# A delta-rule recurrence and a gated MLP on one core: own places for the first gates, and three dense products per batch inside the recurrence where there were five

## The chip, the cores and the metric

The kernel runs on one core of one Trainium2 chip. The metric is the device time of one execution in microseconds (us); it is 695.72 us, the median of three runs of the kernel before. Every duration below comes from a profiled execution of the same kernel.

## The reference

Two stages follow each other. The first is a recurrence over 768 time steps for 4 batches of 8 heads, with a 40x40 state per head:

```python
for t in range(S):
    y[:, :, t] = np.einsum('bhd,bhde->bhe', rt, state)
    Sa = np.einsum('bhde,bhe->bhd', state, at)
    state_decay = state * wt[:, :, None, :] - np.einsum('bhd,bhe->bhde', Sa, bt)
    state = state_decay + np.einsum('bhd,bhe->bhde', vt, kt)
```

Its output, with the heads side by side, is x of shape (4, 768, 320). The second stage is a gated MLP on x: h = gelu(x @ w_in) with 1024 columns, split into u and v of 512; v is normalized over its columns, multiplied with a 768x768 matrix over time (v_s = w_sg v_n + b_sg), and the result is x + (u * v_s) @ w_out.

## The kernel before

**The recurrence in chunks.** Time is cut into 12 chunks of 64 steps. Inside a chunk the steps are solved as a 64x64 triangular system per head. Each chunk has two halves f (two batches each), and each half has two kinds of work.

The *gate* of a half (gate_1 to gate_n, lines 313 to 372) doesn't depend on the state. DVE scans the decays (two scans into `ex`), multiplies them into `at`, and forms `kb` in two parts (a reciprocal, a scan and a product each). PE then multiplies `kb` with `at` into `ab` (gate_s) and transposes `kb` into `kt` (gate_t); ACT copies the negated blocks of `ab` into `nts` (gate_n) and `kt` into `kbt` (gate_k), and DVE masks `ab` back into `at` (gate_a). The inputs of a gate, `main`, have two buffers; gate_3's end releases the load for the gate after next.

The *inverse* of the triangular blocks is made for a whole group of chunks: DVE transposes `nts` into `n` in 32x32 blocks (inv_in), POOL does 58 small multiplications and additions into `tg` and `x`, one column after the other (inv_sub), DVE does the last two columns (inv_end) and transposes `x` into `x1z` (inv_turn). The groups are chunk 0, chunk 1, and then pairs (2, 3), (4, 5) up to (10, 11). `n` has one buffer, so the next group's transposition follows the last group's end.

The *chain* of a chunk (inv_back, inv_g, inv_x, chain1 to chain5) needs that inverse and the state of the chunk before. It runs over PE, ACT and DVE in turn (`xt`, `ru`, `us`, `vu`, `ut`, `pq`, `pqs`, `sp`, `sc`, `yp`, `yt`), and stores the chunk of x to DRAM (`xd`).

**The order is written out by hand.** Every piece of this work has a position, a number. YC gives the position of a chunk's chain, YG the origin of its gates, GATE the offsets of a gate's eleven pieces, YI and INV (INV1 for single chunks) those of a group's inverse. `at_` collects the pieces, in_order sorts them and holds a piece back while the PSUM bank that it would take is in use; each engine then issues its instructions in that order, and the DMA queue SP likewise. A position is thus no time: it says only what stands ahead of what.

**The dense products.** A v-product takes 128 rows of x and the v-half of w_in. Both operands are split into two fp32r parts (`xh`, `xl`; `wvh`, `wvl`), and eight matmuls of 512 columns add up in one bank. Before the change five of the six v-products of each batch are laid into the recurrence: as soon as two chunks of x are done, fill_x loads them (`xf`), fill_split (ACT) and fill_low (POOL) split them (`xfh`, `xfl`), fill_v multiplies (PE, bank `hf`), and fill_out copies the raw product (ACT, `hv`) and stores it to DRAM (`hd`). fill_low also stores the split x to DRAM (`xhd`, `xld`). LASTF is their number, FILL their offsets in a chunk. The v-weights are loaded and split ahead of them, in six pieces at the positions DEC (wstep, line 1050): a load, an activation on ACT, four integer operations on DVE, a copy on ACT, and three subtractions, on DVE for one piece and on POOL for the next.

**The dense half.** Behind the recurrence run issues the rest: u-products (`hu`), the remaining v-products (`hv`), products over time (`sg`) and output products (`op`), by the list FIRSTS for batch 0 and SEQ for each batch. For a v-product that is done already it loads the raw product and does only the gelu and the normalization. GELU, normalization and gates are on ACT, DVE and POOL (`p`, `v`, `bs`, `vh`, `vl`, `g`, `gy`, `gx`), and follow a product by one or two products (later, tick). At a batch's beginning split_x makes the split x of the next batch: for its first 640 columns it loads `xhd` and `xld`, for the last 128 it splits on ACT and DVE. PF are the positions at which batch 0's five products get their gelu while the recurrence still runs.

Of the kernel before, what the change touches and what calls it, by code (L numbers as in the profile page):

```python
# [34 lines left out]
HI_MIN = float(np.uint32(896 << 20).view(np.float32))  # L35
HI_MAX = float(np.uint32(1151 << 20).view(np.float32))
WARM = 14
WARMS = ((-4.831, 8), (-4.331, 8))
BLANKS = -21.0
ZEROS = -36.0  # L40
LOADS = -24.0
PER = 25.5
LATE = 2.5
STORE = 1.5
GATE = ((-101.908, -100.107, -99.028, -96.184, -97.801, -95.604, -92.188, -90.251, -93.577, -91.478, -91.823),
    (-93.163, -92.271, -89.673, -85.987, -88.462, -85.151, -80.147, -78.616, -83.325, -79.712, -81.287))
CHAIN = ((0.0, 1.942, 2.468, 5.095, 5.152, 6.489, 14.151, 16.047, 17.757, 7.942, 9.521, 12.185, 14.84, 17.073,
    19.654), (11.001, 12.574, 2.94, 4.267, 13.405, 14.279, 15.32, 18.186, 26.426, 16.496, 19.044, 24.204, 26.192,
    29.01, 31.005))
YC = (0, 27.5, 81.0, 106.5, 132.0, 157.5, 183.0, 208.5, 234.0, 259.5, 285.0, 310.5)  # L50
YG = (35.908, 55.908, 81.0, 106.5, 132.0, 157.5, 183.0, 208.5, 234.0, 259.5, 285.0, 310.5)
YI = (-3.831, 23.669, 81.0, 132.0, 183.0, 234.0, 285.0)
GATEE = {(0, 0): "VG", (0, 1): "GG"}
GROUPS = ((0,), (1,), (2, 3), (4, 5), (6, 7), (8, 9), (10, 11))
LAST = 2
NBANK = 6
INV = (-61.011, -53.011, -50.811, 0.759, -6.51, -5.143)
INV1 = (-44.0, -29.3, -27.1, 0.429, -2.0, -1.3)
BACK = (-3.831, -0.954, -1.454, -2.595, -0.449, 1.071, 3.249)
END_GT = 232.184  # L60
END_IW = 279.907
END_RING = 292.105
END_IV = 314.249
CG = 0.7978845608028654
G1 = 0.044715
PIN = 232.194
DSTEP = ((-8.5, -1.0, 0.0, 0.7, 1.4, 2.4), (-8.5, -1.0, 0.0, 0.7, 1.4, 2.4))
DSTEPF = (-2.5, -0.5, 0.0, 0.7, 1.4, 2.4)
DEC = (5.0, 15.0, 25.0, 35.0, 45.0, 55.0, 241.194, 247.194, 253.194, 259.194, 265.194, 271.194)
GE = "VV"  # L70
FILL = ((-9.701, 2.299, 2.749, 5.899, 8.777), (3.497, 15.497, 15.947, 19.922, 22.61))
FILLG = True
LASTF = 5
PX = 314.449
PXS = 314.459
PV = 292.205
PS = 338.954
PL = 331.954
PF = (303.0, 308.0, 313.0, 318.0, 323.0)
PH = 9  # L80
FILLERS = ("v0", "v1", "v2", "v3", "v4")
FIRSTS = ("u1", "u0", "u2", "u3", "v5", "u4", "u5", "u6", "u7")
SEQ = ("s1", "s2", "s0", "s3", "s4", "v0", "s5", "v1", "o0", "o1", "o2", "s6", "s7", "v2", "u0", "v3", "u1", "v4",
    "v5", "o3", "o5", "o4", "u2", "u3", "u4", "u5", "u7", "u6")
XS = 0
REST = 8
HL = 2
SGS = (5, 3, 5, 6, 7, 8, 8, 11, 10, 11, 12, 11)
PO = 232.204
DECO = (277.194, 283.194, 289.194, 295.194, 301.194, 307.194, 313.194, 319.194)  # L90
# [102 lines left out]
def attention(tc, a, xd, flag, keep, ps, mlp=None):  # L193
# [4 lines left out]
    with ExitStack() as ctx:  # L198
# [419 lines left out]
            at_(LOADS, load_rv, 0, f)  # L618
        for c in range(NCH):
            for f in range(2):  # L620
                y, n = YG[c], GATE[f]
                at_(y + n[0], gate_1, c, f, 0)
                at_(y + n[1], gate_1, c, f, 1)
                at_(y + n[2], gate_2, c, f, E={"V": V, "G": G}[GATEE.get((c, f), GE)[0]])
                at_(y + n[3], gate_c, c, f)
                for i in range(2):
                    at_(y + n[4 + i], gate_3, c, f, i, E={"V": V, "G": G}[GATEE.get((c, f), GE)[1]])
                for g, p in zip((gate_t, gate_k, gate_s), n[6:]):
                    at_(y + p, g, c, f)
# [56 lines left out]
class Mlp:  # L686
# [3 lines left out]
    def __init__(self, tc, ps, xd, w_in, w2, g_ln, wst, b_sg, w_out, decays, out):  # L690
# [3 lines left out]
        self.V, self.A, self.G, self.T, self.Q = engines(tc)  # L694
        self.ctx = ExitStack()
        self.vn, self.us, self.gs, self.xf = {}, {}, {}, {}
        self.sb, self.done, self.hd, self.xhd, self.xld = None, set(), None, None, None
        self.n, self.todo, self.plan = 0, [], None

    def pool(self, nm, side):  # L700
# [170 lines left out]
        for k in range(2):  # L871
            Q.dma_start(out=t[64 * k:64 * k + 64, 2, c], in_=self.xd[b, 256:320, c])

    def split_cols(self, t, h, l):
        self.A.copy(out=h, in_=t)
        self.V.tensor_tensor(out=l, in0=t[:, 0:2], in1=h[:, 0:2].bitcast(F32), op=ALU.subtract)
        self.V.tensor_tensor(out=h[64:128, 2], in0=t[64:128, 2], in1=h[64:128, 2].bitcast(F32), op=ALU.subtract)

    def split_x(self, b, n):
        e = 128 * LASTF  # L880
        if (b, 0) not in self.done:
            c = slice(384 * n, 384 * n + 384)
# [158 lines left out]
    def side(self):  # L1041
# [44 lines left out]
    def run(self, ahead, verdict=None):  # L1086
# [94 lines left out]
def attention_then_gated_mlp(tc, ins, out):  # L1181
    nc = tc.nc
    a = ins
    with ExitStack() as ctx:
# [8 lines left out]
        part.xhd = dr.tile([B, 128, 3, S], F32, name="xhd")  # L1193
        part.xld = dr.tile([B, 128, 2, S], F32, name="xld")
# [64 lines left out]
```

## Time and profile before

| | us |
|---|---|
| median of three runs | 695.72 |
| the three runs | 695.24, 695.72, 705.01 |
| the profiled execution | 702.58 |
| its span, first to last instruction | 700.5 |
| its busy time: PE, DVE, POOL, ACT | 558.7, 486.9, 351.9, 336.1 |

The profiled execution is one run of the program, and its span is 2.1 us shorter than its time. PE is the matmul engine (PEld its weight loads), DVE the vector engine, ACT the scalar engine, POOL the engine for simple operations on SBUF, SP the engine that issues DMAs. A row names the tiles without their buffer numbers, `out<-in`. Busy time is a sum over stages with different limits, so it is read by stage: the first gates and inverses (0 to 174 us), the chunks 2 to 9 (174 to 405), the last two chunks (405 to 475), the dense half (475 to the end).

### The profile page before, as it was taken

The numbers are of one execution on the slowest core, as the hardware profiler recorded it, in microseconds if no ns is written. First come the engines' busy times: TensorE is split into PE (matmuls) and PEld (weight loads), VectorE is DVE, ScalarE is ACT, GpSimd is POOL, SyncE is SP. The second block draws the span as 40 slices with busy tenths as digits, with TensorE's granted clock in tenths as the row PEclk, the third lists the DMA queues.
The fourth block names the chain that finished last, engine by engine and source line by source line (L and its number), as shares of the span: only waits on it lengthen the run. The fifth ranks groups of instructions, "written<-read, shape, count | busy, mean of one in ns | idle before, by whom it ended". The sixth has DMA issues, their size and how long they took to land.

```text
span 700.5 us, 25303 instructions
## 1 busy us (share of the span) xinstructions
PE 558.7 (80%) x10710; PEld 509.5 (73%) x10710; DVE 486.9 (70%) x950; ACT 336.1 (48%) x736; POOL 351.9 (50%) x596
## 2 busy tenths in 40 slices
PE   4452766835989989798986979679779999899996
PEld 4352765724878878677875768469779998799995
DVE  5673677766656867765868756537568889969942
ACT  3330547424565767566675566625334434434510
POOL 3186842945585487177566843323244333334331
PEclk8556666765789999899998899779899999999999
DMA  5460262333256565765555556655601465232001
GB/s 185 119 167 6 80 151 83 103 92 106 80 152 163 150 173 149 200 155 138 155 149 153 140 159 167 181 176 159 219 30 63 145 222 153 89 132 73 29 23 39
DMA packets 87138, 89.50 MB, mean 128 GB/s; under 512 B 38280, under 2 KB 69000, under 8 KB 85000
## 3 DMA queue, kind: packets, MB, share of 16 engines
q1 hardware_dynamic: 87016, 87.79, 44.3%
q8 instruction: 86, 1.41, 0.9%
q14 instruction: 36, 0.29, 0.1%
HBM read 68.10 MB, written 19.66 MB: 125 GB/s over the span
## 4 chain that ended last, share of the span: by engine, by line
PE 44%; DVE 16%; issue 6%; ACT 4%; POOL 2%; DMA 2%; SPq 1%; POOLq 0%; ACTq 0%; DVEq 0%
PE sg L179 10%; PE hf L179 5%; PE yp L179 5%; PE op L179 3%; PE ru L179 3%; DVE v L179 3%; PE ut L179 3%; PE pq L179 3%; PE sp L179 2%; DVE p L179 2%; PE ab L179 2%; DVE cv L179 2%; PE xp L179 2%; DVE g L179 2%; PE kt L179 2%
## 5 line engine op out<-in xcount | busy, mean ns | idle before, releaser
L179 POOL TENSOR_TENSOR tg<-x,n 128x135 f32<-128x135 f32 (+25 forms) x203 | 104.1, 513 | 79.9 <-issue 30.7
L179 POOL TENSOR_TENSOR x<-x,tg 128x135 f32<-128x135 f32 (+25 forms) x203 | 106.1, 523 | 15.8
L179 PE MATMUL ab<-at,kb 64*64 64x64 f32 x1536 | 42.4, 268 | 56.3 <-DVE fixed L179 22.7
L179 PEld LDWEIGHTS ab<-at,kb 64*64 64x64 f32 x1536 | 36.9, 175 | 61.0 <-issue 31.8
L179 ACT ACTIVATE nts<-ab 32x512 f32<-32x512 f32 x96 | 46.3, 483 | 57.3 <-PE ab L179 54.4
L179 PE MATMUL sg<-wsh,vh 128*128 128x384 f32 x192 | 66.7, 347 | 5.8 <-ACT wsh L179 3.4
L179 PE MATMUL sg<-wsl,vh 128*128 128x384 f32 x192 | 67.1, 350 | 4.0 <-POOL wsl L179 2.9
L179 POOL TENSOR_TENSOR gx<-g,gy 128x384 fp32r<-128x384 f32 x32 | 34.0, 1066 | 71.6 <-ACT gy L179 71.6
L179 PE MATMUL sg<-wsh,vl 128*128 128x384 f32 x192 | 66.7, 347 | 0.9 <-POOL vl L179 0.9
L179 DVE TENSOR_TENSOR at<-ab,mask 64x512 f32<-64x512 f32 x48 | 32.2, 678 | 42.9 <-ACT nts L179 32.7
L179 POOL TENSOR_TENSOR rs<-rs,mhalf 128x1 f32<-128x1 f32 x24 | 14.9, 624 | 76.0 <-DVE rs L179 72.4
L179 ACT CAST gy<-g 128x384 fp32r<-128x384 f32 x32 | 16.4, 514 | 62.2 <-DVE g L179 59.4
L179 PEld LDWEIGHTS sg<-wsh,vh 128*128 128x128 f32 x192 | 37.2, 194 | 7.0 <-ACT wsh L179 4.4
L179 ACT CAST vh<-v 128x512 fp32r<-128x512 f32 x24 | 14.6, 619 | 56.4 <-DVE v L179 56.4
L179 PEld LDWEIGHTS sg<-wsl,vh 128*128 128x128 f32 x192 | 37.1, 193 | 5.8 <-POOL wsl L179 3.5
L179 DVE TENSOR_TENSOR pqs<-pq,mask 128x512 f32<-128x512 f32 x48 | 30.7, 681 | 14.5 <-PE pq L179 14.5
L179 DVE TENSOR_TENSOR yt<-yp,ex 128x256 f32<-128x256 f32 x48 | 18.1, 417 | 31.5 <-PE yp L179 30.2
L179 PEld LDWEIGHTS sg<-wsh,vl 128*128 128x128 f32 x192 | 37.3, 194 | 2.1 <-POOL vl L179 2.0
L179 PE MATMUL kt<-ident,kb 128*128 128x128 f32 x192 | 35.2, 342 | 2.8 <-issue 2.8
L179 PE MATMUL ut<-ident,vu 64*64 64x64 f32 x768 | 32.2, 235 | 6.1 <-ACT vu L179 6.1
L179 PEld LDWEIGHTS ut<-ident,vu 64*64 64x64 f32 x768 | 28.1, 146 | 11.3 <-ACT vu L179 8.7
L179 POOL TENSOR_TENSOR vl<-v,vh 128x512 fp32r<-128x512 f32 x24 | 31.6, 1320 | 8.8 <-ACT vh L179 8.8
(154 smaller groups left out, 1554.8 us busy)
## 6 DMA issues: line engine op xcount, KB each, us to landing
main<-main SPq DMA_DIRECT2D x44, 321.4 KB
hd<-hv SPq DMA_DIRECT2D x20, 256.0 KB
v<-hd SPq DMA_DIRECT2D x20, 256.0 KB
vu<-vs SPq DMA_DIRECT2D x24, 160.0 KB
vs<-vb SPq DMA_DIRECT2D x24, 160.0 KB
rt<-rt SPq DMA_DIRECT2D x48, 80.0 KB
vut<-vt SPq DMA_DIRECT2D x48, 80.0 KB
xd<-yt SPq DMA_DIRECT2D x96, 40.0 KB
```

The lines of the kernel that those rows point to most:

```text
L179: return self.tc.keep_in_program_order(f(*a, **k))
```

## The change

**The first gates.** The gates of the chunks 0 to 3 get positions of their own (GATE0), 9.2 apart, from -50.0 to 14.4, all with the same offsets; in these kt comes before ab. The gates of chunk 0 lose the parts that they had on POOL (GATEE is empty). The inverses of chunk 0, chunk 1 and the pair (2, 3) get own positions too (INV0), and the chains move (YC, YG).

**The weights.** All six v-weight pieces do their three subtractions on DVE, at new positions; their loads stand 6.5 units earlier relative to their use (DSTEPF from -2.5 to -9.0).

**The dense products.** LASTF goes from 5 to 3: three v-products per batch stay in the recurrence, v3 and v4 of each batch go into the dense half. The copies `xhd` and `xld` in DRAM go. split_x splits all 384 columns of each half on ACT and POOL.

```diff
-BLANKS = -21.0
-ZEROS = -36.0
+BLANKS = -55.0
+ZEROS = -35.0
...
+GATE0 = {(0, 0): (-50.0, (0, 0.6, 1.2, 2.0, 2.1, 3.5, 5.0, 6.2, 6.1, 10.6, 7.4)), (0, 1): (-40.8, (0, 0.6, 1.2, 2.0,
...
-YC = (0, 27.5, 81.0, 106.5, 132.0, 157.5, 183.0, 208.5, 234.0, 259.5, 285.0, 310.5)
+YC = (2.231, 31.531, 75.831, 101.331, 126.831, 152.331, 177.831, 203.331, 228.831, 254.331, 279.831, 305.331)
...
-GATEE = {(0, 0): "VG", (0, 1): "GG"}
+GATEE = {}
...
-INV1 = (-44.0, -29.3, -27.1, 0.429, -2.0, -1.3)
+INV0 = {0: (-38.7, -31.7, -29.5, 0.443, -3.5, -2.8), 1: (-9.4, -2.4, -0.2, 0.443, 25.8, 26.5), 2: (19.9, 26.9, 29.1,
+    0.702, 70.1, 70.8)}
...
-DSTEPF = (-2.5, -0.5, 0.0, 0.7, 1.4, 2.4)
+DSTEPF = (-9.0, -0.5, 0.0, 0.7, 1.4, 2.4)
...
-LASTF = 5
+LASTF = 3
...
-PF = (303.0, 308.0, 313.0, 318.0, 323.0)
+PF = (302.831, 308.831, 314.831, 320.831, 326.831)
...
-FIRSTS = ("u1", "u0", "u2", "u3", "v5", "u4", "u5", "u6", "u7")
+FIRSTS = ("u1", "u0", "v0", "v1", "u2", "v2", "u3", "v3", "v4", "v5", "u4", "u5", "u6", "u7")
...
-                y, n = YG[c], GATE[f]
+                y, n = GATE0.get((c, f)) or (YG[c], GATE[f])
...
-    def split_cols(self, t, h, l):
+    def split_x(self, b, n):
+        c = slice(384 * n, 384 * n + 384)
+        t, h, l = self.xts[b % 2][:, :, c], self.xh[:, :, c], self.xl[:, :, c]
         self.A.copy(out=h, in_=t)
-        self.V.tensor_tensor(out=l, in0=t[:, 0:2], in1=h[:, 0:2].bitcast(F32), op=ALU.subtract)
-        self.V.tensor_tensor(out=h[64:128, 2], in0=t[64:128, 2], in1=h[64:128, 2].bitcast(F32), op=ALU.subtract)
-
-    def split_x(self, b, n):
-        e = 128 * LASTF
-        if (b, 0) not in self.done:
-            c = slice(384 * n, 384 * n + 384)
-        elif n == 0:
-            self.Q.dma_start(out=self.xh[:, :, 0:e].bitcast(F32), in_=self.xhd[b, :, :, 0:e])
-            self.Q.dma_start(out=self.xl[:, :, 0:e].bitcast(F32), in_=self.xld[b, :, :, 0:e])
-            return
-        else:
-            c = slice(e, S)
-        self.split_cols(self.xts[b % 2][:, :, c], self.xh[:, :, c], self.xl[:, :, c])
+        self.G.tensor_tensor(out=h[64:128, 2], in0=t[64:128, 2], in1=h[64:128, 2].bitcast(F32), op=ALU.subtract)
+        self.G.tensor_tensor(out=l, in0=t[:, 0:2], in1=h[:, 0:2].bitcast(F32), op=ALU.subtract)
...
-        c = slice(128 * k, 128 * k + 128)
-        self.Q.dma_start(out=self.xhd[b, :, :, c], in_=h.bitcast(F32))
-        self.Q.dma_start(out=self.xld[b, :, :, c], in_=l.bitcast(F32))
...
-                steps[k] = self.split64(*self.weights_in()[k], HF // 2, self.G if k % 2 and k < 6 else self.V)
+                steps[k] = self.split64(*self.weights_in()[k], HF // 2, self.V)
...
-        names = [*FIRSTS] if ahead else [*FILLERS, *FIRSTS]
+        names = [x for x in FIRSTS if x not in FILLERS[:LASTF]] if ahead else [*FILLERS, *FIRSTS]
```

The rows below show how this moves instructions. On DVE, near the beginning of the program, this stands before ahead of the first 32x32 transposition; ex_131 is the scan of the fourth gate, at_140 and ab_332 and ab_333 belong to the third:

```order
L179 TENSOR_TENSOR kb<-main_96,fixed_95 128x2x4x64
L179 SCALAR_TENSOR_TENSOR ex_131<-main_97,fixed_94 128x260 x2
L179 TENSOR_TENSOR at_140<-ab_332,mask 64x8x64
L179 TENSOR_TENSOR at_140<-ab_333,mask 64x8x64
L179 TENSOR_SCALAR call<-ex_131 128x8
L179 TENSOR_TENSOR at_141<-main_97,ex_131 128x8x64
L179 STREAM_TRANSPOSE n<-nts_103 128x32x32
```

In the changed kernel this stands on DVE at the same place; ex_127, at_137 and main_95 are the second gate's, at_136 and ab_218 and ab_219 the first's, and ex_128 is the third's:

```order
L185 TENSOR_TENSOR at_136<-ab_218,mask 64x8x64
L185 TENSOR_TENSOR at_136<-ab_219,mask 64x8x64
L185 RECIPROCAL fixed_92<-call 128x4
L185 SCALAR_TENSOR_TENSOR fixed_93<-main_95,fixed_92 128x260
L185 TENSOR_TENSOR kb<-main_95,fixed_93 128x2x4x64
L185 RECIPROCAL fixed_92<-call 128x4
L185 SCALAR_TENSOR_TENSOR fixed_93<-main_95,fixed_92 128x260
L185 TENSOR_TENSOR kb<-main_95,fixed_93 128x2x4x64
L185 STREAM_TRANSPOSE n<-nts_101 128x32x32
L185 SCALAR_TENSOR_TENSOR ex_128<-main_94,fixed_92 128x260 x2
```

The transposition of chunk 0 moves from behind the third gate and the fourth's scans to right behind the second gate, whose `nts` it reads.

On POOL, in the substitution of the pair (2, 3), this stands before; the stg and wvl rows are the subtractions of a weight piece:

```order
L179 TENSOR_TENSOR x<-x,tg 128x5x27
L179 TENSOR_TENSOR stg_1539<-stg_1539,stg_1515 128x256
L179 TENSOR_TENSOR stg_1476<-stg_1476,wvh 128x256
L179 TENSOR_TENSOR wvl<-stg_1476,stg_1539 128x256
L179 TENSOR_TENSOR tg<-x,n 128x156
```

And this in the changed kernel, at the same step of the substitution:

```order
L185 TENSOR_TENSOR tg<-x,n 128x135
L185 TENSOR_TENSOR x<-x,tg 128x5x27
L185 TENSOR_TENSOR tg<-x,n 128x156
L185 TENSOR_TENSOR x<-x,tg 128x6x26
L185 TENSOR_TENSOR tg<-x,n 128x175
```

The weight pieces leave POOL: the substitutions of the first three groups stand there without anything between. On DVE there are 58 instructions between the transposition of `nts` for chunk 1 and the end of its substitution, and 87 between that of the pair (2, 3) and the end of its own.

On PE, where the recurrence ends, this stands before (hf is the last product inside the recurrence, hu a u-product, hv a v-product):

```order
L179 MATMUL hf<-wvh,xfl 128x512 x2
L179 MATMUL hu<-xh,wuh 128x384 x3
L179 MATMUL hu<-xh,wul 128x384 x3
L179 MATMUL hu<-xl,wuh 128x384 x2
```

Behind the fourth u-product the changed kernel has three v-products in a row, where one stood:

```order
L185 MATMUL hv<-wvh,xh 128x512 x3
L185 MATMUL hv<-wvl,xh 128x512 x3
L185 MATMUL hv<-wvh,xl 128x512 x2
L185 MATMUL hv<-wvh,xh 128x512 x3
L185 MATMUL hv<-wvl,xh 128x512 x3
L185 MATMUL hv<-wvh,xl 128x512 x2
L185 MATMUL hv<-wvh,xh 128x512 x3
```

The hf products of k = 3 and 4, eight in all, are gone from the chunks 8 to 11 and from behind the last, and eight hv products have come, two per batch.

## Rows read from the trace of the kernel before

**Rows 1.** Windows by stage: us, busy (count) of PE, PEld, DVE, ACT, POOL, clock, DMA.

```profile
174.00:405.00 231.00, 202.21 (x5980) 179.99 (x5976) 167.42 (x315) 144.24 (x323) 150.24 (x265) 0.91 0.57 150
...
405.00:475.00 70.00, 53.40 (x1403) 45.39 (x1402) 36.47 (x88) 37.87 (x90) 23.62 (x40) 0.85 0.60 170
...
475.00:700.50 225.50, 206.86 (x1123) 197.41 (x1121) 167.92 (x323) 84.58 (x172) 79.91 (x79) 0.97 0.33 105
```

**Rows 2.** Timeline of DVE and POOL, 6 to 36 us: start, length, instruction.

```profile
6.07 1.28 DVE L179 TENSOR_TENSOR_SCAN ex<-main,fixed 128x260 f32<-128x260 f32 x2 [1.81 <-DMA main<-first]
...
24.42 0.15 DVE L179 TENSOR_SCALAR call<-ex 128x8 f32<-128x8 f32 x1
...
27.69 0.69 DVE L179 TENSOR_TENSOR kb<-main,fixed 128x512 f32<-128x512 f32 x1
...
32.89 2.07 DVE L179 STREAM_TRANSPOSE n<-nts 128x1024 f32<-128x1024 f32 x1
...
35.04 0.24 POOL L179 TENSOR_TENSOR tg<-x,n 128x31 f32<-128x31 f32 x1 [14.46 <-DVE fixed L179]
```

**Rows 3.** Windows between the 32x32 transpositions, columns as in rows 1.

```profile
65.20:110.80 45.60, 29.69 (x826) 27.48 (x828) 34.14 (x68) 22.79 (x51) 24.66 (x61) 0.65 0.37 100
...
110.80:169.40 58.60, 35.11 (x904) 31.15 (x904) 39.61 (x81) 26.78 (x62) 39.53 (x64) 0.69 0.40 105
```

**Rows 4.** Chain of waits, 183 to 187 us, and a group of ACT by line.

```profile
183.47 1.71 PE ab L179 x58
...
185.18 1.90 PE kt L179 x8
...
L179 ACT ACTIVATE nts<-ab 32x512 f32<-32x512 f32 x96 | 46.3, 483 | 57.3 <-PE ab L179 54.4 <-PE yp L179 1.7
```

**Rows 5.** Waits of DVE, 110.8 to 169.4 us: total, times, longest.

```profile
DVE stg L179 <- ACT stg L179: 7.4, 2, 6.2
...
DVE at L179 <- ACT nts L179: 4.0, 3, 3.4
```

**Rows 6.** Waits of POOL, 60 to 174 us, and its timeline.

```profile
POOL stg L179 <- ACT wvh L179: 15.9, 3, 8.1
...
152.20 0.72 POOL L179 TENSOR_TENSOR stg<-stg,stg 128x256 f32<-128x256 f32 x1 [8.14 <-ACT wvh L179]
...
154.23 0.73 POOL L179 TENSOR_TENSOR wvl<-stg,stg 128x256 fp32r<-128x256 f32 x1
```

**Rows 7.** Timeline of DVE and POOL: one instruction twice, and POOL beside it.

```profile
110.04 0.41 DVE L179 TENSOR_TENSOR stg<-stg,wvh 128x256 f32<-128x256 f32 x1
...
139.29 0.89 POOL L179 TENSOR_TENSOR tg<-x,n 128x256 f32<-128x256 f32 x1
...
139.59 0.87 DVE L179 TENSOR_TENSOR stg<-stg,wvh 128x256 f32<-128x256 f32 x1
```

**Rows 8.** Chain of waits: the eight matmuls of one inner, one later product.

```profile
428.88 2.04 PE hf L179 x8
...
480.62 1.88 PE hv L179 x8
```

**Rows 9.** Waits of PE, 405 to 475 us, and the timeline of ACT.

```profile
PE us L179 <- ACT xt L179: 6.0, 2, 5.8
...
439.86 0.26 ACT L179 ACTIVATE cv<-stg 128x64 f32<-128x64 f32 x1 [3.50 <-DMA stg<-w_out]
```

**Rows 10.** Windows late in the dense half, columns as in rows 1.

```profile
575.00:600.00 25.00, 23.41 (x127) 21.68 (x126) 23.96 (x49) 9.25 (x18) 7.70 (x9) 1.00 0.38 115
...
600.00:625.00 25.00, 22.68 (x120) 22.15 (x119) 20.00 (x45) 10.62 (x22) 10.70 (x11) 0.93 0.46 155
```

**Rows 11.** Groups of POOL by line, 475 us to the end; one wait of the chain.

```profile
L179 POOL TENSOR_TENSOR gx<-g,gy 128x384 fp32r<-128x384 f32 x32 | 34.0, 1066 | 71.6 <-ACT gy L179 71.6
...
L179 POOL TENSOR_TENSOR vl<-v,vh 128x512 fp32r<-128x512 f32 x21 | 27.7, 1327 | 8.8 <-ACT vh L179 8.8
...
499.95 4.03 DMA xt<-xd
```

More of the change, by code (lines that the diff above doesn't have):

```diff
@@ L37 @@
 WARM = 14
-WARMS = ((-4.831, 8), (-4.331, 8))
-BLANKS = -21.0
-ZEROS = -36.0
-LOADS = -24.0
+WARMS = ((-2.6, 8), (-2.1, 8))
+BLANKS = -55.0
+ZEROS = -35.0
+LOADS = -12.0
 PER = 25.5
@@ L49 @@
     29.01, 31.005))
-YC = (0, 27.5, 81.0, 106.5, 132.0, 157.5, 183.0, 208.5, 234.0, 259.5, 285.0, 310.5)
-YG = (35.908, 55.908, 81.0, 106.5, 132.0, 157.5, 183.0, 208.5, 234.0, 259.5, 285.0, 310.5)
-YI = (-3.831, 23.669, 81.0, 132.0, 183.0, 234.0, 285.0)
-GATEE = {(0, 0): "VG", (0, 1): "GG"}
+YC = (2.231, 31.531, 75.831, 101.331, 126.831, 152.331, 177.831, 203.331, 228.831, 254.331, 279.831, 305.331)
+YG = (45.508, 65.508, 85.508, 105.508, 126.831, 152.331, 177.831, 203.331, 228.831, 254.331, 279.831, 305.331)
+GATEE = {}
 GROUPS = ((0,), (1,), (2, 3), (4, 5), (6, 7), (8, 9), (10, 11))
@@ L57 @@
 INV = (-61.011, -53.011, -50.811, 0.759, -6.51, -5.143)
-INV1 = (-44.0, -29.3, -27.1, 0.429, -2.0, -1.3)
+INV0 = {0: (-38.7, -31.7, -29.5, 0.443, -3.5, -2.8), 1: (-9.4, -2.4, -0.2, 0.443, 25.8, 26.5), 2: (19.9, 26.9, 29.1,
+    0.702, 70.1, 70.8)}
 BACK = (-3.831, -0.954, -1.454, -2.595, -0.449, 1.071, 3.249)
[L60 to L63, printed above, removed]
+END_GT = 227.015
+END_IW = 274.738
+END_RING = 286.936
+END_IV = 309.08
 CG = 0.7978845608028654
 G1 = 0.044715
-PIN = 232.194
+PIN = 227.025
 DSTEP = ((-8.5, -1.0, 0.0, 0.7, 1.4, 2.4), (-8.5, -1.0, 0.0, 0.7, 1.4, 2.4))
-DSTEPF = (-2.5, -0.5, 0.0, 0.7, 1.4, 2.4)
-DEC = (5.0, 15.0, 25.0, 35.0, 45.0, 55.0, 241.194, 247.194, 253.194, 259.194, 265.194, 271.194)
+DSTEPF = (-9.0, -0.5, 0.0, 0.7, 1.4, 2.4)
+DEC = (10.0, 22.0, 34.0, 46.0, 58.0, 70.0, 236.025, 242.025, 248.025, 254.025, 260.025, 266.025)
 GE = "VV"
@@ L72 @@
 FILLG = True
-LASTF = 5
[L74 to L78, printed above, removed]
-PF = (303.0, 308.0, 313.0, 318.0, 323.0)
+LASTF = 3
+PX = 309.28
+PXS = 321.28
+PV = 287.036
+PS = 333.785
+PL = 326.785
+PF = (302.831, 308.831, 314.831, 320.831, 326.831)
 PH = 9
 FILLERS = ("v0", "v1", "v2", "v3", "v4")
-FIRSTS = ("u1", "u0", "u2", "u3", "v5", "u4", "u5", "u6", "u7")
+FIRSTS = ("u1", "u0", "v0", "v1", "u2", "v2", "u3", "v3", "v4", "v5", "u4", "u5", "u6", "u7")
 SEQ = ("s1", "s2", "s0", "s3", "s4", "v0", "s5", "v1", "o0", "o1", "o2", "s6", "s7", "v2", "u0", "v3", "u1", "v4",
@@ L88 @@
 SGS = (5, 3, 5, 6, 7, 8, 8, 11, 10, 11, 12, 11)
-PO = 232.204
-DECO = (277.194, 283.194, 289.194, 295.194, 301.194, 307.194, 313.194, 319.194)
+PO = 227.035
+DECO = (272.025, 278.025, 284.025, 290.025, 296.025, 302.025, 308.025, 314.025)
 DSTEPO = (-8.5, -1.0, 0.0, 0.7, 1.4, 2.4)
@@ L644, in attention @@
         for g in GROUPS:
-            z, v = YI[GROUPS.index(g)], INV if len(g) > 1 else INV1
+            z, v = (0, INV0[g[0]]) if g[0] in INV0 else (YC[g[0]], INV)
             at_(z + v[0], inv_load, g)
@@ L696, in __init__ @@
         self.vn, self.us, self.gs, self.xf = {}, {}, {}, {}
-        self.sb, self.done, self.hd, self.xhd, self.xld = None, set(), None, None, None
+        self.sb, self.done, self.hd = None, set(), None
         self.n, self.todo, self.plan = 0, [], None
@@ L1079, in side @@
         at(PS, self.split_x, 0, 1)
-        for k, p in enumerate(PF):
+        for k, p in enumerate(PF[:LASTF]):
             at(p - PH, self.load_h, 0, k)
@@ L1192, in attention_then_gated_mlp @@
         part.hd = dr.tile([B, LASTF, 128, HF], F32, name="hd")
-        part.xhd = dr.tile([B, 128, 3, S], F32, name="xhd")
-        part.xld = dr.tile([B, 128, 2, S], F32, name="xld")
         verdict = attention(tc, a, xd, flag, keep, ps, part)
```

5 rows, old and new, of the table GATE0 are left out of this document.

## The prediction

> **What bounds the kernel now.** I read the windows by stage first, then the timeline where the first substitution begins, then the waits of the engines in each stage, and last the chain of waits.
>
> In the dense half PE is busy 206.9 of 225.5 us: work added to PE there is paid nearly in full. In chunks 2 to 9 it is busy 202.2 of 231, also close to the bound; in the last two chunks only 53.4 of 70 [rows 1]. The first 174 us are another matter. There a serial path decides: DVE transposes `nts`, POOL substitutes, DVE finishes and transposes back, three times over (chunk 0, chunk 1, the pair), before chunk 2 can begin. The first transposition starts at 32.9 and POOL only at 35.04, after an idle time of 14.5 [rows 2]; the second starts at 65.2, the third at 110.8, and the third substitution's end is finished by DVE at 169.4 (the bounds of the windows in [rows 3]).
>
> All sums are against the profiled execution, 702.58 us. The median of the runs is 695.72, 1% lower; I carry the difference in us over to it.
>
> **The change part by part.**
>
> *The first gates and inverses.* A gate costs DVE about 5.2 us up to its second `kb`: 1.28 for the scans, and 3.96 from `call` at 24.42 to the end of `kb` at 28.38 [rows 2]. Now `kt` stands before `ab`. Behind the second `kb` PE has half of kt (1.90 for all eight), then ab (1.71 for 58 of 64), and ACT has four copies of 0.48 [rows 4]: 0.95 + 1.9 + 1.9 = 4.8 us until `nts` is whole. The first gate starts at 6.1, so its `kb` ends at 11.2 and its copies at 16.0. The second gate's kb parts wait behind the first gate's masks (one 0.7 behind the last copy) and take 3.2: 19.9, and its `nts` is whole at 24.7. There the first transposition starts, 8 earlier than now.
>
> From the first transposition to the second it is 32.3 now. The substitution between them stays; a gate's start, two masks and `x1z` come between its end and the next transposition, and the memsets go out of it. I add 2: the second starts at 59, 6 earlier. From there DVE issues 58 instructions before it may finish the second substitution. At the mean of this stretch, 34.14 us for 68 [rows 3], these are 29.1, and I add 4.0 of waits for `nts`, as the next stretch has [rows 5], with 2.1 for the transposition itself: 94. Finishing, `x1z` and a scan take 2.4: the third transposition starts at 97, 14 earlier.
>
> The third substitution takes 56 us now, from 113 to 169.4. It contains 12 of the 15.9 us in which POOL waits for `wvh`, that is for a weight piece whose first step waits for its load, and two pieces of up to 2.8 of its own (152.20 to 154.96) [rows 6]. Without them it is 39. On DVE stand 87 instructions, at 39.61 us for 81 [rows 3] 42.5, with 4.0 of waits [rows 5] 46.5. So DVE, not POOL, is late next: 97 + 2.1 + 46.5 = 146, plus some 3 for waits that the denser order brings, 149. Against 169.4 that is **20 us less**. If POOL alone decides, it is 97 + 2 + 39 = 138 (31 less). If DVE takes as long as it does now, 58.6, it is 157 (12 less). I take 20, since the 7.4 us that DVE waits for the weights' ACT step [rows 5] should go: the loads stand 6.5 units earlier.
>
> *Three pieces' subtractions go from POOL to DVE.* They are in the 87. The row shows a price that the mean may hide: the same subtraction takes 0.41 us with POOL idle and 0.87 beside POOL's multiplication, which itself takes 0.89 [rows 7]. Nine such instructions at 0.46 more are 4 us, and the head would give 16. The Trainium skill (SBUF — State Buffer, "SBUF: two separate sides") has a stronger rule: the port pair that DVE and GpSimd share goes to one instruction for its whole length, for a DVE instruction with two SBUF inputs as well, and the other engine fully blocks. The trace agrees that both stretch (0.87 and 0.89). By that rule each of the nine could wait out one POOL instruction of 0.89, 8 us, and the head would give 12. I leave the mean in, as it was taken with POOL at work.
>
> *Eight inner products go.* An hf product is 2.04 us of PE [rows 8], so 16.3. Three lie in chunks 8 and 9, where PE is busy 88% of the time, five in the last two chunks and behind them, at 76% [rows 1]: 6.1 x 0.88 + 10.2 x 0.76 = 13; with the gelu of two products fewer on ACT and DVE there I take **14 less**. The lower bound is 0: PE waits 6.0 us for `xt` there, because ACT, which works in order, waits 3.5 for a w_out piece's load [rows 9], and if such waits set these chunks, freed PE time buys nothing. The upper bound is 16.3 + 6.0 = 22. The copies to `xhd` and `xld` leave SP's queue; I cost that at nothing, since it only helps these waits.
>
> *Eight outer products come.* An hv product is 1.88 us [rows 8]: **15 more**. In batch 2 to 3 PE idles 1.6 and 2.3 us of two windows, 3.9 together [rows 10], which can hide two products. Against that the splits: POOL does 768 columns in place of 512 at 1.33, 2.0 by that, and 64 rows of 384 at about 1.07 [rows 11], 3.1 per half, 6.1 per batch turn, behind ACT, which waits 4.0 for the x load [rows 11]. The next batch's first product needs them only five sg products later, some 16 us. So it is hidden, and if not it is up to 6 a turn. Bounds: 15 - 4 = 11, and 15 + 4 x 6 = 39.
>
> The sum: -20 - 14 + 15 = -19. 702.58 - 19 = 683.6, and against the median 695.72 - 19 = **677**.
>
> **The rivals.**
>
> *DVE holds the head, and the last chunks wait for other things.* DVE's queue grows by three weight pieces' subtractions and two gates' products ahead of the third substitution's end. If it takes 58.6 us as now, the head gives 12; if ACT's waits set chunks 10 and 11, the recurrence gives 5, from chunks 8 and 9. -12 - 5 + 15 = -2: 694. For it: ACT's wait of 3.5 and PE's of 6.0 [rows 9]. Against it: POOL's 15.9 us of waits do go.
>
> *POOL paces, and all frees up.* The head gives 31, the recurrence 20, and the windows of [rows 10] hide 4 of the 15: -40, 656. For it: the 12 us of waits that stood in POOL's way [rows 6]. Against it: 87 DVE instructions at half a microsecond.
>
> *The splits stall the dense half: slower.* At each of the four starts of a batch POOL's 6.1 us stand in front of the next `gx` and the weight split `wsl`, behind ACT's wait for the x load [rows 11]. If PE waits them out, the dense half costs 15 + 24 = 39. With the head at 20 and the recurrence at 14 this is +5: 701. It decides from (34 - 15) / 4 = 4.8 us of stall per start. For it: the chain of waits already runs through that load. Against it: the 16 us of sg products ahead of the first use.
>
> **How the numbers follow.** Forecast 0.5, its own range 666 to 690; the first rival 0.22; the second 0.13; the third 0.10; 0.05 for what I don't see. A measurement of this kernel tells about 2% from no change, 14 us: faster means under 682. Of the forecast's half 0.40 lies below that. Faster: 0.40 + 0.13 + 0.04 of the first rival and 0.02 of the rest, 0.59. Slower by over 2% (above 709) is the third rival with 8 us of stall per start, and part of the rest: 0.08. The remaining 0.33 is within 2%. The range goes from the second rival's 658 to 698, which leaves out most of the third rival and a little at the lower end.
>
> **What would show it.** Right: the first POOL substitution starts near 27, the 32x32 transpositions stand near 25, 59 and 97, chunk 2's `x1z` starts near 150, POOL waits for no `wvh`; DVE, not POOL, ends the wait before the third `x1z`. The stretch from there to the last `yp` is some 14 shorter than 305, the dense half near 240 with PE still over 90% busy. Wrong: a third transposition later than 105, or DVE with over 55 us between it and the finish; last chunks as long as now; a dense half over 250, with waits of PE for `xl`, `vl` or `wsl`.

## The result, and the profile after

The changed kernel takes 675.18 us (median of four runs, 673.05 to 682.72) against 696.64 for the kernel before in the same comparison: a ratio of 0.969, 95% interval [0.960, 0.978]. In a second comparison (e11) it was 675.30 against 701.63, 0.960 [0.953, 0.968]. The forecast was 677. The profiled execution took 675.57, its span is 673.5; against the 702.58 of before these are 27.0 less, where the sum had 19. The medians lie 21.5 apart: the profiled execution of before took 6 us more than the median of its runs, so the stages below hold to a few us only.

The windows by stage show where. First those of the kernel after, columns as in [rows 1] and GB/s last: the bounds are the starts of the three 32x32 transpositions, of `x1z` of the pairs (2, 3) and (10, 11), and the end of the last `yp`.

```profile
0.00:25.20 25.20, 13.90 (x172) 12.09 (x172) 13.92 (x29) 8.29 (x16) 5.45 (x25) 0.70 0.63 201
25.20:58.80 33.60, 16.40 (x274) 13.77 (x276) 25.45 (x48) 10.83 (x22) 22.72 (x58) 0.56 0.42 101
58.80:98.30 39.50, 25.47 (x760) 22.58 (x754) 31.93 (x66) 21.07 (x48) 22.71 (x58) 0.79 0.43 109
98.30:147.00 48.70, 33.25 (x959) 30.12 (x955) 46.19 (x95) 25.68 (x58) 34.09 (x58) 0.75 0.46 116
147.00:375.20 228.20, 201.74 (x6022) 181.28 (x6020) 171.45 (x324) 146.13 (x327) 148.56 (x260) 0.87 0.50 129
375.20:434.40 59.20, 50.28 (x1361) 46.31 (x1361) 27.62 (x73) 29.68 (x73) 15.71 (x26) 0.64 0.35 95
434.40:673.50 239.10, 222.99 (x1190) 212.78 (x1186) 172.15 (x329) 93.47 (x181) 104.06 (x97) 0.96 0.24 72
```

And the kernel before by the same three later bounds (its head is in [rows 2, 3]; `x1z` at 170.1):

```profile
170.10:405.20 235.10, 204.23 (x6040) 181.80 (x6040) 171.45 (x321) 145.41 (x324) 150.44 (x265) 0.91 0.56 148
405.20:473.00 67.80, 51.20 (x1394) 43.73 (x1393) 35.23 (x85) 37.36 (x89) 23.42 (x40) 0.85 0.59 170
473.00:700.50 227.50, 208.86 (x1132) 199.06 (x1130) 168.96 (x325) 85.09 (x173) 79.91 (x79) 0.97 0.33 106
```

| | before | after | difference | forecast |
|---|---|---|---|---|
| start to chunk 2's `x1z` | 170.1 | 147.0 | -23.1 | -20 |
| from there to the last `yp` | 302.9 | 287.4 | -15.5 | -14 |
| from there to the end | 227.5 | 239.1 | +11.6 | +15 |

PE's 202 of 228 us and 50 of 59 look like stages bound by PE. The column of the clock says otherwise: in the last two chunks it is 0.64, against 0.85 before, and PE is busy 50.3 us with less to multiply than in the 51.2 of before. That row was the hint that the middle term may not be what the prediction took it for. Nor does PE wait for `xt` there any longer [rows 9]; its waits of the last two chunks, 375.2 to 434.4 us, begin with

```profile
PE ut L185 <- ACT vu L185: 3.3, 3, 1.4
PE gp L185 <- DVE x1z L185: 2.7, 1, 2.7
PE pq L185 <- ACT vut L185: 2.5, 1, 2.5
```

The head went as the prediction had it. DVE's and POOL's timeline of the kernel after:

```profile
25.19 2.09 DVE L185 STREAM_TRANSPOSE n<-nts 128x1024 f32<-128x1024 f32 x1 [5.20 <-ACT nts L185]
27.42 0.24 POOL L185 TENSOR_TENSOR tg<-x,n 128x31 f32<-128x31 f32 x1 [20.95 <-DVE n L185]
...
58.77 2.07 DVE L185 STREAM_TRANSPOSE n<-nts 128x1024 f32<-128x1024 f32 x1
98.29 2.10 DVE L185 STREAM_TRANSPOSE n<-nts 128x1024 f32<-128x1024 f32 x1
100.53 0.24 POOL L185 TENSOR_TENSOR tg<-x,n 128x31 f32<-128x31 f32 x1 [12.38 <-DVE n L185]
...
154.15 0.24 POOL L185 TENSOR_TENSOR tg<-x,n 128x31 f32<-128x31 f32 x1 [15.07 <-DVE n L185]
```

All of POOL's waits from 60 to 152 us, and DVE's from 98.3 to 147 (total, times, longest):

```profile
POOL tg L185 <- DVE n L185: 12.4, 1, 12.4
POOL tg L185 <- DVE fixed L185: 6.4, 1, 6.4
...
DVE pqs L185 <- PE pq L185: 0.9, 1, 0.9
DVE stg L185 <- ACT stg L185: 0.4, 1, 0.4
```

POOL no longer waits for `wvh` [rows 6]; ahead of each substitution it waits for DVE. DVE is busy 46.2 of the 48.7 us of the third stretch and waits 1.3.

The comparisons below leave out disturbed runs, so a ratio is not quite the quotient of two medians; the profiled execution of e11 was disturbed and its stages are not used, and that of before counts as disturbed too. The stages of before stand all the same, because kernels that keep them show them again: e2 a head of 170.3, e1 a recurrence of 299.0 and a dense half of 230.3, where before has 170.1, 302.9 and 227.5.

### The profile page after: what moved, and what is told of

Same layout as the page of the kernel before. It is cut to its first block, busy times and chain, and to the rows that moved or that the text cites. A ratio compares the mean times of both kernels' runs of the same rounds, so it can differ in the third digit from the quotient of the medians.

```text
span 673.5 us, 25104 instructions
## 1 busy us (share of the span) xinstructions
PE 564.0 (84%) x10710; PEld 518.9 (77%) x10710; DVE 488.7 (73%) x956; ACT 335.1 (50%) x724; POOL 353.3 (52%) x582
## 4 chain that ended last, share of the span: by engine, by line
PE 55%; DVE 21%; ACT 8%; issue 7%; POOL 5%; DMA 3%; SPq 0%; POOLq 0%; DVEq 0%; ACTq 0%
PE sg L185 11%; PE yp L185 6%; PE ut L185 4%; PE op L185 4%; PE sp L185 4%; PE pq L185 4%; PE hf L185 4%; PE ru L185 4%; PE ab L185 3%; DVE v L185 3%; PE hu L185 2%; PE kt L185 2%; PE xp L185 2%; DVE p L185 2%; POOL x L185 2%
## 5 line engine op out<-in xcount | busy, mean ns | idle before, releaser
L185 ACT ACTIVATE nts<-ab 32x512 f32<-32x512 f32 x96 | 46.5, 484 | 32.5 <-PE ab L185 31.3
L185 PEld LDWEIGHTS kt<-ident,kb 128*128 128x128 f32 x192 | 26.3, 168 | 37.1 <-issue 26.4
L185 PE MATMUL ab<-at,kb 64*64 64x64 f32 x1536 | 38.7, 262 | 10.8 <-DVE fixed L185 9.6
L185 PE MATMUL ut<-ident,vu 64*64 64x64 f32 x768 | 36.6, 247 | 11.4 <-ACT vu L185 7.4
L185 PEld LDWEIGHTS ab<-at,kb 64*64 64x64 f32 x1536 | 34.8, 173 | 14.3 <-issue 7.0
L185 PEld LDWEIGHTS ut<-ident,vu 64*64 64x64 f32 x768 | 31.3, 157 | 16.7 <-ACT vu L185 9.7
L185 DVE SCALAR_TENSOR_TENSOR g<-sg,gl,bt 128x384 f32<-128x384 f32 x32 | 19.6, 612 | 28.3 <-PE sg L185 15.7
```

Of the source, the lines that this page charges most:

```text
L185: return self.tc.keep_in_program_order(f(*a, **k))
```

## The experiments

Twelve runs were made, each beside the kernel before on its chip. "Head", "recurrence" and "dense" are the three stages of the table above, in the profiled execution.

| run | median | ratio to before, 95% | head | recurrence | dense |
|---|---|---|---|---|---|
| e1 gates alone | 682.96 | 0.977 [0.971, 0.984] | 150.7 | 299.0 | 230.3 |
| e2 dense part alone | 697.99 | 0.995 [0.990, 0.999] | 170.3 | 276.1 | 240.1 |
| e3 pieces on POOL | 675.61 | 0.969 [0.962, 0.976] | 153.3 | 280.0 | 239.0 |
| e4 late loads | 684.52 | 0.982 [0.976, 0.988] | 153.2 | 284.5 | 239.8 |
| e5 splits on DVE | 673.15 | 0.975 [0.955, 0.994] | 150.3 | 284.3 | 236.9 |
| e6 four products | 670.04 | 0.969 [0.953, 0.986] | 149.4 | 280.0 | 234.1 |
| e7 products without use | 672.17 | 0.972 [0.957, 0.988] | 149.5 | 281.7 | 238.4 |
| e8 `ab` first | 671.03 | 0.970 [0.956, 0.984] | 147.1 | 277.6 | 238.8 |
| e9 five products, no copies | 673.14 | 0.962 [0.953, 0.970] | 149.4 | 285.2 | 234.7 |
| e10 three edits | 667.44 | 0.952 [0.944, 0.961] | 149.0 | 283.6 | 232.7 |
| e11 the changed kernel again | 675.30 | 0.960 [0.953, 0.968] | | | |
| e12 e9 with the stores | 684.05 | 0.975 [0.969, 0.980] | 149.1 | 297.8 | 234.5 |

The four runs of one kernel spread by 0.7 to 1.6%, so no difference of medians under 4 us is read as one. The stages are those of one execution each, and they spread too. The changed kernel and six others with the same gates, pieces and loads (e1, e5, e6, e7, e9, e12) start `x1z` between 147.0 and 150.7. The change, e3, e4 and e8 have the same work in the recurrence, and it takes 277.6 to 287.4 us, with a clock of 0.64 to 0.81 in the last two chunks. The profiled executions of e2, e4, e6 and e8 were the fastest of their kernels, 5 to 10 us under the medians beside them.

### e1 and e2: each half of the change by itself

e1 is the changed kernel with before's dense part:

```diff
-LASTF = 3
+LASTF = 5
-PXS = 321.28
+PXS = 309.29
...
+        self.Q.dma_start(out=self.xhd[b, :, :, c], in_=h.bitcast(F32))
+        self.Q.dma_start(out=self.xld[b, :, :, c], in_=l.bitcast(F32))
```

together with before's split_x, split_cols and FIRSTS, and PF from 297.8 on in steps of 5. e2 is the opposite: before with LASTF = 3, FIRSTS, split_x and fill_low of the change, and PXS = 326.449, PF = (308.0, 314.0, 320.0).

> The new positions of the first gates, inverses and weight pieces, with the dense part as before: five inner products per batch, the split copies fetched from DRAM. If the three terms add up as the two traces show them (head 23 us shorter, first `x1z` of chunk 2 to the last `yp` 15 to 18 shorter, dense half 13.5 longer, of which the last two belong together), this kernel keeps the head's 23 (chunk 2's `x1z` near 147), its dense half is near 226 again, and it comes out near 676, within 4 us of the changed kernel. Rival: the gates alone free nothing that lasts, because five inner products fill the chunks whose gates came early, and some 8 of the 23 are given back in chunks 2 to 9: near 685.

> The kernel before with only the dense part changed: three inner products per batch, ten more outer ones less two, the split of x by ACT and POOL. If the terms add up, its head is as before (chunk 2's `x1z` near 170), the recurrence behind it 10 to 15 us shorter than 303, the dense half 13 longer: 692 to 697, no difference that can be told from the kernel before. Rival: the 15 us that the recurrence won in the changed kernel came from the gates of chunks 2 and 3, which now stand ahead of it, and not from the products: then the recurrence is shorter by under 6 here and the time is 705 to 708.

e1's head is near 150 and e2's 170.3, so the head belongs to the gates with their weight pieces. The recurrence goes the other way: 299.0 in e1 (302.9 before), 276.1 in e2, so its gain belongs to the dense part, not to the gates. e1's dense half is back at 230. The gates alone are worth 2.3% of the time (16 of 701 us), the dense part alone 0.5%; together 0.972, which agrees with the change's 0.969. The two halves add up, and nearly all of the gain is the head. e1 itself came out at 683, nearer to its rival's 685 than to 676, but not by its rival's reason: the dense part is worth 4 us by e2 and 8 by e1, more than the sum left for it (14 won, 15 lost). Nor were 8 us given back in the chunks 2 to 9: e1 takes 231.9 for them, before 235.1.

### e3 and e4: what ended POOL's waits

```diff
-                steps[k] = self.split64(*self.weights_in()[k], HF // 2, self.V)
+                steps[k] = self.split64(*self.weights_in()[k], HF // 2, self.G if k % 2 and k < 6 else self.V)
```

> The changed kernel with the subtractions of three of the six inner weight pieces back on POOL, their loads still early. If the earlier loads ended POOL's waits for `wvh`, POOL waits under 3 us for it, loses some 6 to 8 us to the pieces themselves, which it has to spare, and DVE issues nine instructions fewer: 672 to 677. Rival: the move to DVE ended them; then POOL waits 10 us or more for `wvh` again, chunk 2's `x1z` starts at 155 or later, and the time is 682 to 687.

```diff
-DSTEPF = (-9.0, -0.5, 0.0, 0.7, 1.4, 2.4)
+DSTEPF = (-2.5, -0.5, 0.0, 0.7, 1.4, 2.4)
```

> The changed kernel with the loads of the six inner weight pieces 2.5 units ahead of their first step, as before, in place of 9, and their subtractions on DVE. If the lead of the loads matters, DVE waits 7 us or more for the pieces' ACT step (it waits 4.9 in the changed kernel), chunk 2's `x1z` starts 4 to 8 us later than 147, and the time is 679 to 684. Rival: the move to DVE alone ended the waits: under 2 us of difference, 674 to 677.

POOL's two longest kinds of wait in e3, 60 to 174 us, and DVE's in e4, 90 to 155:

```profile
POOL stg L185 <- DMA vut<-vt: 10.1, 1, 10.1
POOL stg L185 <- ACT stg L185: 9.8, 2, 6.2
```

```profile
DVE stg L185 <- ACT stg L185: 7.5, 4, 3.5
```

In e3 POOL stands in front of the pieces for 19.9 us again, though their loads are early: so it was the move to DVE that took POOL out of the way of the weights, as its rival said. `x1z` is at 153.3, 3 to 6 later than in the seven kernels named above, but the time is the first theory's, 675.6, and shows nothing of the late head. In e4 the third stretch is 56.5 us (96.7 to 153.2) with DVE busy 45.6 of them, where the changed kernel has 46.2 of 48.7, and from 90 to 155 us DVE waits 7.5 for the pieces, where the changed kernel waits 2.6. The time is 684.5, 9 more than the changed kernel's on the same chip (e11). So the early loads are needed. That the pieces must leave POOL too is not shown: the head of e3 is as late as that of e4, and yet its time is the change's; why the two times differ stays open. With either of the two taken back, 17 of the head's 23 us remain; both together were not taken back.

### e5, e6, e8: the splits, the number of products, the order in the gate

e5: in split_x both subtractions on self.V in place of self.G. e6: LASTF = 4. e8, in all eight entries of GATE0:

```diff
-5.0, 6.2, 6.1, 10.6, 7.4
+6.1, 7.4, 5.0, 10.6, 6.2
```

> The changed kernel with the two subtractions of every split of x on DVE in place of POOL. If POOL's splits are hidden, as the prediction had it, nothing is won: DVE is busy over 90% of the stretch from 550 to 575 us, gets some 2.5 us more per batch start, and the time is 675 to 682. Rival, the prediction's slower case: PE waits for POOL's splits at the batch starts; then DVE's quicker ones (0.6 in place of 2.2 us for the 768 columns) save 2 us or more per start, and the time is 667 to 671.

> The changed kernel with four inner products per batch in place of three. If a product costs PE the same inside and outside, the recurrence gets 4 x 2.0 x 0.85 = 7 longer, the dense half 4 x 1.88 = 7.5 shorter, and the time is 672 to 679. Rival: two products fewer outside also end part of the 6 us that PE waits between 453 and 464 us for the normed `vh` and `vl` of the outer products; then the dense half is 10 or more shorter and the time is 668 to 671.

> The changed kernel with `ab` and its copies to `nts` ahead of `kt` and its copies in the eight early gates. If DVE's path through the gates sets the head, each gate's `nts` is whole some 2 us earlier, the three 32x32 transpositions start near 23, 55 and 93 in place of 25.2, 58.8 and 98.3, chunk 2's `x1z` near 141, and the time is 668 to 672. Rival: the head is shorter but the recurrence gives it back, because the chain of chunks 0 and 1 waits for the later `kt`, or because PE's work behind `x1z` is the same: 673 to 677.

e5's 673 lies between its two cases, as far as can be told level with the change, and the slower rival of the prediction falls: DVE takes 0.96 to 1.67 us for the 768 columns, POOL 1.81 to 2.18, and the dense half is 2 shorter. e6's 670 falls into its rival's range, 668 to 671, but not for its rival's reason: its dense half is 5 shorter, not 10, and the recurrence did not get longer for the four products. In e8 the first two transpositions start at 21.2 and 54.7, 4 earlier than in the change, but the third at 96.9 and `x1z` at 147.1, where the change has 147.0 and e10, with the same order, 149.0: the six of the forecast did not come. DVE's longest kind of wait between the second and the third transposition, in e8 and then in the change, shows where the first 4 went, to the weight pieces:

```profile
DVE stg L184 <- ACT stg L184: 8.8, 3, 3.9
...
DVE stg L185 <- ACT stg L185: 4.4, 4, 1.8
```

The time, 671.0, is the one expected all the same; in the profiled execution it is made by a recurrence of 277.6, which no step of mine foretold.

### e7: eight products that nothing reads

```diff
+        def idle_v():
+            o = self.ps("hf")
+            for i in range(8):
+                self.T.matmul(o, lhsT=self.wvh[:, i % 3, 0:128], rhs=self.wvh[:, i % 3], start=(i == 0), stop=(i == 7), skip_group_check=True)
+
+        for k in (3, 4):
+            for b in range(B):
+                n = 2 * k + 2 + (b + 1) // 2
+                at(YC[min(n, NCH - 1)] + PER * max(0, n - NCH + 1) + FILL[1 - b % 2][3], idle_v)
```

> The changed kernel with eight more inner products of weights by weights laid where the kernel before has its fourth and fifth; nothing reads them, and ACT, DVE, POOL and the DMA queues get no more work. If the 15 us that the recurrence won are PE's time of the eight products, they come back here: 8 x 2.04 x 0.85 = 14, 687 to 691. Rival: PE's clock is granted lower where the products went (0.66 behind 375 us, against 0.85 in the last two chunks before); then products that keep PE at work bring the clock there to 0.8 or more and pay half of themselves back: 678 to 683.

672.2, and a recurrence of 281.7: eight products more cost nothing that can be measured. Both expectations fall, the rival in its size only. Windows of 8 us of the changed kernel, columns as before:

```profile
342.00:350.00 8.00, 3.25 (x96) 2.90 (x96) 6.64 (x12) 2.69 (x6) 7.21 (x11) 0.67 0.39 103
350.00:358.00 8.00, 6.09 (x110) 5.45 (x114) 5.67 (x10) 5.99 (x14) 7.14 (x11) 0.50 0.23 66
...
366.00:374.00 8.00, 8.00 (x156) 7.69 (x156) 5.52 (x15) 4.20 (x11) 1.33 (x2) 0.50 0.29 80
...
398.00:406.00 8.00, 8.00 (x198) 7.47 (x200) 4.15 (x17) 3.25 (x10) 1.03 (x4) 0.50 0.23 61
```

And of e7:

```profile
342.00:350.00 8.00, 7.94 (x262) 6.88 (x257) 7.31 (x15) 2.57 (x6) 7.22 (x11) 1.00 0.44 125
350.00:358.00 8.00, 1.89 (x62) 1.76 (x63) 6.66 (x12) 4.47 (x10) 7.22 (x11) 0.75 0.24 71
...
366.00:374.00 8.00, 7.66 (x285) 7.06 (x282) 7.66 (x20) 5.22 (x14) 1.81 (x5) 1.00 0.58 160
...
398.00:406.00 8.00, 7.49 (x246) 6.33 (x238) 4.74 (x16) 5.21 (x12) 1.24 (x3) 1.00 0.48 117
...
376.20:431.20 55.00, 47.22 (x1393) 41.35 (x1393) 27.74 (x73) 29.88 (x73) 16.38 (x28) 0.91 0.37 100
```

Without the products PE has a gap (3.25 of 8 us busy), after it the clock is at 0.50, its lower level of 1.2 GHz, and later windows are full at that level (8.00 busy). e7 has a gap too, a little later (1.89 busy), but from 366 on it runs at 1.00, the level of 2.4 GHz, and does 285 matmuls in 7.66 us where the other does 156 in 8.00 (not all of one shape). Over the last two chunks e7 has 0.91 against 0.64, and PE is busy 47.2 us with the products against 50.3 without. The changed kernel is the low end here: e2 and e8 have 0.81 there without such products, PE is busy 43.6 and 43.7 us, and the two chunks take 53.9 and 53.5 us, where e7 takes 55.0 and the change 59.2.

### e9 and e12: what did make the recurrence longer

If the eight products cost no time, something else that went with them cost the 15. e9 is the changed kernel with LASTF = 5 alone (no copies to DRAM, x split anew); e12 is e9 with the two stores per product that before has, and no reader:

```diff
+        c = slice(128 * k, 128 * k + 128)
+        self.Q.dma_start(out=self.xhd[b, :, :, c], in_=h.bitcast(F32))
+        self.Q.dma_start(out=self.xld[b, :, :, c], in_=l.bitcast(F32))
```

> The changed kernel with five inner products per batch, and x split anew as in the changed kernel, so without the split copies to and from DRAM that the run of the gates alone still had. Products that nothing reads cost nothing, so something else that goes with the inner products made the recurrence longer. If it was the copies to DRAM on SP's queue, the stretch from chunk 2's `x1z` to the last `yp` stays at 280 to 288 here, against 299 with the copies, the dense half comes down to 227 to 232, and the time is 660 to 668. Rival: it was the products' own work on ACT (the split, the copy of `hv`, the gelu), behind which `rhsb` and `xt` wait in order; then the stretch is 295 to 300 again, PE waits 6 us or more for `rhsb` and `xt` in the last two chunks, and the time is 676 to 683.

> The five inner products of the run before, with the stores of their split halves to DRAM put back and nothing that reads them; the split of x and the order of the dense part stay as they are there. If the stores on SP's queue are what made the recurrence longer, the stretch from chunk 2's `x1z` to the last `yp` is 295 to 300 in place of 285, PE waits 6 us or more for `xt` and `rhsb` in the last two chunks, and the time is 682 to 690. Rival: it was the other things that the gates alone had as before, the place of the split of x and of the gelus of the inner products; then the stretch stays at 283 to 289 and the time at 671 to 677.

e9: 285.2 for the recurrence, like the change's 287.4 with three products. e12: 297.8, like e1's 299.0, and 684 in place of 673. All four times of e12 (681.5 to 686.9) lie above all four of e9 (671.3 to 679.5); the kernel before took 701.4 and 701.6 beside them. e9's time missed its 660 to 668, because its dense half gave 4.4 back in place of 7 to 12. ACT's and PE's waits in the last two chunks, first e9:

```profile
ACT cv L185 <- DMA stg<-w_out: 0.8, 1, 0.8
```

then e12, ACT, PE and SP's queue:

```profile
ACT cv L185 <- DMA stg<-w_out: 7.7, 2, 4.8
...
PE us L185 <- ACT xt L185: 3.6, 2, 3.5
...
SPq L185 <- POOL xfh L185: 5.7, 3, 4.8
```

One such wait of e12 in its timeline, from SP to PE:

```profile
403.80 0.58 SPq L185 DMA_DIRECT2D xhd<-xfh  x1
404.42 1.16 SPq L185 DMA_DIRECT2D xld<-xfl  x1
405.68 1.21 SPq L185 DMA_DIRECT2D vu<-vs  x2
...
410.69 0.44 SPq L185 DMA_DIRECT2D stg<-w_out  x1
...
414.32 0.26 ACT L185 ACTIVATE cv<-stg 128x64 f32<-128x64 f32 x1 [4.83 <-DMA stg<-w_out]
414.61 0.43 ACT L185 COPY rhsb<-ru 128x320 f32<-128x320 f32 x1
...
415.34 1.17 ACT L185 COPY xt<-xp 32x512 f32<-32x512 f32 x2
...
415.96 0.43 PE L185 MATMUL us<-rhsb,xt 64*64 64x40 f32 x2 [3.47 <-ACT xt L185]
```

SP works in order: the stores stand in its queue (0.58 and 1.16 here, and elsewhere they wait 5.7 for POOL's split); the w_out piece is issued behind them, ACT waits 4.83 for it, `rhsb` and `xt` stand behind that on ACT, and PE waits 3.47 for `xt`. It is the pair of waits of [rows 9], which e9 doesn't have. That the stores make the recurrence longer is shown: with them it is 297.8 to 302.9 (e12, e1, before), without them 276.1 to 287.4 in ten kernels. The 12.6 is the difference of two single executions. How it comes about is shown in part only. SP issues without a break from 399.6 us to the w_out piece, and the two stores are 1.7 us of that, less than the 4.83 of the wait. And the last two chunks, e12 and then e9, differ less in PE's idle time (10.7 and 9.4 us) than in its busy time at a lower clock, for the same work:

```profile
379.00:446.90 67.90, 57.18 (x1400) 48.10 (x1399) 34.21 (x85) 38.22 (x91) 26.61 (x41) 0.78 0.51 144
...
374.70:434.60 59.90, 50.49 (x1395) 42.81 (x1393) 34.67 (x85) 39.30 (x91) 28.24 (x44) 0.86 0.51 139
```

The clock is 0.57 from 415 us on in e12, behind the wait shown. How much is the queue's order, how much the stores' traffic (the DMA share from chunk 2 to 9 is 0.58 in e12, 0.52 in e9) and how much the clock was not tried.

### e10 and e11: a faster version

e10 is the changed kernel with the edits of e5, e6 and e8 together.

> Three edits together that were each level or a little faster alone: four inner products per batch, `ab` ahead of `kt` in the eight early gates, the splits of x on DVE. If their gains add up (5, 4 and 2 us against the changed kernel), 663 to 667; if they are the spread of the runs, 671 to 676.

> The changed kernel as it is, beside these runs: 671 to 678. It tells how far its stages differ between two profiled executions: chunk 2's `x1z` at 147 before, the last `yp` at 434.4.

On one chip e10 takes 667.4 (665.8 to 672.6) and the changed kernel 675.3 (672.2 to 683.2): 1.2% less, the fastest kernel of the study. It lies between its two cases, nearer to the gains adding up: 8 us of the 11. The intervals of the two ratios, [0.944, 0.961] and [0.953, 0.968], still overlap.

## Why the prediction was right, and for which term by chance

**Head, -20: right, by its own steps.** `n` at 25.2, 58.8 and 98.3 (24.7, 59, 97), POOL at 27.42 (27), `x1z` at 147.0 (150 at the latest count), no wait for `wvh`, and DVE nearly full at the end, not POOL. The step of 46.5 us for DVE, 42.5 of work and 4.0 of waits, measured 44.1 and 1.3 (46.2 less the transposition's 2.1); the price of a denser order (3) was hardly asked. In the eight further kernels with these gates, pieces and loads (e1, e5 to e10, e12; in e8 and e10 with `ab` first) `x1z` starts between 147.1 and 150.7, 19 to 23 ahead of before. The dearer price of nine subtractions beside POOL did not show: in the kernel after

```profile
L185 DVE TENSOR_TENSOR stg<-stg,wvh 128x256 f32<-128x256 f32 x6 | 2.9, 480 | 0.0
```

all six have a mean of 0.48 us, near the 0.41 of [rows 7] and not its 0.87; the other two subtractions of a piece have 0.43 and 0.58. What did become dearer are the pieces' integer operations, 0.64 and 0.40 us each in place of 0.46 and 0.34, some 2 us in all. The Trainium skill (SBUF — State Buffer, "SBUF: two separate sides") has the loser of the shared port pair wait for the whole of the other's instruction; by that the head would have given 12, and it gave 23. One sum of the head is off: the rival's 157 adds the transposition's 2.1 to a stretch of 58.6 that contains it, and is 155.6.

**Recurrence, -14: right in size by luck, wrong in cause.** The step was "An hf product is 2.04 us of PE [rows 8], so 16.3", weighted with PE's busy share. That PE is busy 76 or 88% of a stretch doesn't make its work the price: eight products that nothing reads added nothing that shows (e7), five real ones in place of three nothing (e9). The 15 came from what the prediction costed "at nothing", the copies to `xhd` and `xld` that leave SP's queue: 12.6 of recurrence and 11 of time (e12 less e9). And 15.5 is the short end of what the spread allows: e3, e4 and e8, with the same work there, are 18 to 25 below before. The lower bound of 0 with its reason, PE's waits behind ACT's wait for w_out, named the right rows; what was missed is that the change takes a cause of those waits away.

**Dense half, +15: 11.6, near in size, by its steps in part only.** Between the two profiles it splits as the prediction did: PE is busy 223.0 us against 208.9, 14.1 more, eight products of 1.88 being 15.0; the idle time became 2.5 less. The weights' split no longer makes PE wait (in before `sg` waits 3.4 for `wsh` and 4.0 for `wsl`); in its place `sg` waits for the normed outer products. The rule "over 90% busy" held, 93%. The later runs do not bear this split out. e9 and e12 have all eight products back inside and split x anew, and their dense half is 234.7 and 234.5: there the eight are worth 4 to 5 us, not 15. Before and e1 have the same products and load the split x, and theirs is 227.5 and 230.3. So 4 to 7 of the 11.6 came with the new split of x and its place in the order, which the prediction took to be hidden. It shows more as PE's busy time (213.9 and 211.3 against 208.9 and 208.1) than as waits; which step carries it was not tried.

PE's longest kinds of wait in the kernel after, 430 us to the end:

```profile
PE sg L185 <- ACT vh L185: 3.7, 3, 1.9
PE hu L185 <- DVE v L185: 2.4, 2, 1.9
PE sg L185 <- POOL vl L185: 2.4, 3, 1.1
```

**Rivals.** DVE holding the head fell with `x1z` at 147; POOL pacing it (656, in the prediction's range 658) fell, since POOL waits for DVE; the splits' stall fell, since PE waits for no `xl` from 430 us on, and moving them to DVE changed the time by nothing that can be measured (e5).

The total was right within 2 us, partly by luck: the term with the wrong cause had the right size, and a part of the dense half's came from a term that had been taken to be hidden. Had the change kept the copies of its three products, the same working would have given 677 all the same, and after e12 I would expect it to have been too low.

## What to carry to other kernels

A busy engine's work is a price only if the stage ends on it: lay useless copies of that work in, and see whether the time moves, before counting its removal as a gain. In a queue that works in order, a store takes its place, and waits for its data, ahead of every load behind it; look at what stands behind it, and who waits for that, before costing its removal at nothing. Where a long serial head is fed by one engine at 95%, give that engine its inputs early. And test each term by itself: a sum can come out right over two terms whose causes were wrong.

## What the hardware showed that I had not expected

Matmuls in PE's gaps can cost far less than they take by themselves, because PE then runs at a higher clock. The same instructions of the last two chunks take 302 ns (`pq`) and 281 (`yp` from `pqs`) in the changed kernel at a mean clock of 0.64, and 240 and 245 in e7 at 0.91, with 9.6 us of products more. Against the changed kernel the products paid for themselves; against e2 and e8, which have 0.81 there without them, the two chunks are 1 to 2 us longer for the 9.6. So it is no fixed gain, and the clock of such a stage varies between kernels with the same work there.
